# A residual block with tiled fast convolution: where the row transform keeps its scratch, and which adds are done by DMA

## The chip, the cores and the metric

The kernel runs on one core of a Trainium2 chip. A core has five engines that run side by side, each with its own instruction stream: TensorE (matmuls, into PSUM), VectorE (called DVE in the profile), ScalarE (ACT), GpSimd (POOL) and SyncE (SP). SP and POOL issue DMAs; sixteen DMA engines of the core carry them out. The metric is the device time of one execution in microseconds, taken as the median over several runs.

## The reference

The reference is a residual block of a diffusion model: two 3x3 convolutions over 512 channels and a 64x64 image, batch 2, each behind a group normalisation (four groups) and a SiLU. An embedding is added to each channel between the two, and the input at the end.

```python
def conv3(z, w):
    zp = jnp.pad(z, ((0, 0), (0, 0), (1, 1), (1, 1)))
    taps = [jnp.einsum("bchw,oc->bohw", zp[:, :, i:i+H, j:j+W], w[:, :, i, j]) for i in range(3) for j in range(3)]
    ...
h = conv3(_silu(gn(x, g1, be1)), w1)
emb = _silu(t_emb) @ w_emb
h = h + emb.reshape(B, C, 1, 1)
h = conv3(_silu(gn(h, g2, be2)), w2)
return x + h
```

## The kernel before

**The algorithm.** In the vertical direction the convolution is a fast one: four output rows are made from six input rows by six products in place of twelve. So an input tile is first turned, on VectorE and ScalarE, into six *planes* (numbers 0 to 5, 8 rows of 65 elements each, `PL` = 520 elements), each plane is multiplied with its transformed weights on TensorE, and the six products are combined into four output rows. Planes 4 and 5 belong to the *outer rows*: their products are added only to the first and the last of the four output rows. In the horizontal direction some planes have a second fast step, the *nest*: differences of even and odd columns, written to an area of their own (`vnest`).

**Chunks, tiles, units.** The work is cut into eight chunks: layer (2) x image (2) x half of the image (2). A chunk has four input tiles of 128 channels (`ct`) and four units, one for each 128 output channels (`k`). Chunk 0 has no nest (mode N), chunks 1 to 3 have it on planes 0 and 2 (mode 0), chunks 4 to 6 on planes 0 to 3 (mode 1), and chunk 7 on all six. Layer 1's outputs go to a DRAM scratch `h_scr`, layer 2's are added by a DMA from POOL onto `out`, where a DRAM-to-DRAM DMA from SP has put the residual before (the `pre` copies).

**Production.** `prod(c, ct)` (L1163) makes the planes of tile `ct` of chunk `c`, while TensorE works on chunk `c-1`: `load_a` (one of two buffers `AB`), `silu` (ScalarE), then `rows_a` (L624) and `rows_b` (L638). These keep intermediate rows in a scratch `w` of 33 to 34 rows, and write planes 0 to 3 to `X0` or `X1` or to the tile's own area, from where the nest is made. `early` picks one of two orders of the same adds. In the late order planes 4 and 5 first hold a part, and a last add over both planes (1040 elements, the *plane sum*) completes them; where `vacc` is set, that add is an accumulating DMA from POOL inside SBUF. It reads `w`, so `w` can't be written again before it has landed. The scratch is `WB[0]` for all tiles, or one of two (`W2B`) in chunks 5 and 6. The planes and nests of even and odd chunks lie in two areas `VB[0]` and `VB[1]`, `VP` = 4160 elements for each tile; in mode 1 planes 4 and 5 lie elsewhere, in `VX`.

**A unit.** `unit(c, k)` (L823; `unit7` in chunk 7, `last_y` for its last unit) runs the matmuls over the four tiles. ScalarE empties PSUM into `M`, `BT` and the outer-row buffers `OO`; VectorE combines these into the output tile `ys`, one of two. Last come the outer rows: an add of 2 x 520 elements on VectorE (L955), or, where `CFG["oacc"]` of the layer is set, an accumulating DMA from POOL (L953). In layer 1 the tile is then stored, and ScalarE squares and sums it for the next normalisation.

**Order.** Nothing runs in the order of the source. `Plan` collects every operation with a cost, a latency and the ranges that it reads and writes, schedules them (`solve`), and emits them by planned start. So each engine has a fixed order, and an instruction that waits holds up all that is behind it on its engine. A DMA from POOL has a latency of 3.2 us in the plan (L366), beside a time for its size that is reckoned at 150 GB/s when it accumulates.

Of the kernel before, what the change touches and what calls it, by code (L numbers as in the profile page):

```python
# [11 lines left out]
ALU = mybir.AluOpType  # L12
AX = mybir.AxisListType
F32 = mybir.dt.float32
BF16 = mybir.dt.bfloat16
# [162 lines left out]
def _idx(off, dims):  # L178
# [7 lines left out]
RW = 65  # L186
PL = 8 * RW
YF = 4 * PL
AF = 34 * RW
VP = 4160  # L190
KF = 33 * RW
MS = 512
BB, CT, P, NCH, ET = 2, 4, 128, 2, 9
# [6 lines left out]
CFG = {  # L200
    'k0': (D_, D_, D_, D_),
    't0': D_,
    'k': (D_, D_, A_, D_, A_, A_, D_, A_),
    't': (D_, D_, A_, D_, A_, A_, A_, D_),
    's': ((A_, A_, A_), (D_, D_, D_), (D_, A_, A_), (D_, D_, D_), (A_, A_, A_), (A_, A_, D_), (A_, A_, A_), (D_, A_, D_)),
    'oacc': (0, 0),
    'np': 1,
    'pre': 4,
    'wpe': (1, 0, 0, 0),
    'vacc': (1, 0, 0, 1, 0, 1, 1, 1),  # L210
}


# [1 line left out]
def kernel(  # L215
# [14 lines left out]
    o = 0  # L230
    UREG, UM = [], 10304
# [3 lines left out]
    VB = [o, o + 16640 + 2240 + 14928]  # L235
    WB = [o + 16640 + 63]
    Z = o + 16640 + 2240
# [7 lines left out]
    TB = o  # L245
# [7 lines left out]
    X0 = Z + 6912  # L253
    BT0 = Z + 8992
    SD0 = Z + 10016
    O0 = [Z + 11552, Z + 12592, Z + 13632]
    VX = [Z + 16, Z + 6416]
    X1 = Z + 4320
    BT1 = Z + 12880
    W2B = [WB[0], Z + 10721]  # L260
    SD1 = TB

    pool = ctx.enter_context(tc.tile_pool(name="arena", bufs=1))
# [26 lines left out]
    def A(off, dims, dt=None):  # L290
        b = ar[:] if dt is None else ar[:].bitcast(dt)
        n = 1
        for d in dims:
            n *= d[1]
        return R(bass.AP(b.tensor, b.offset + off, [list(b.ap[0])] + [list(d) for d in dims]),
                 ("A", _idx(off, dims)), n)
# [29 lines left out]
    def regs(*rs):  # L326
        return [r.reg if isinstance(r, R) else r for r in rs]

    def tt(out, a, b, op, name=""):
        pl.op("DVE", 0.075 + 0.000521 * out.n, lambda: nc.vector.tensor_tensor(out=out.ap, in0=a.ap, in1=b.ap, op=op),  # L330
              regs(a, b), regs(out), name)
# [23 lines left out]
    def scal(eng, out, a, s, name=""):  # L355
        if eng == "ACT":
            act(out, a, ACT.Copy, scale=s, name=name)
        else:
            ts(out, a, s, name)

    def dma(out, in_, r, w, nbytes, name="", sw=False, acc=False, after=None, lat=None):
        rate = 0.15 if acc else 0.37
        kw = {"accum_op": ALU.add, "max_dma_last_dim": 2080} if acc else {}
        eng = nc.gpsimd if sw else nc.sync
        pl.op("DMA", nbytes / rate * 1e-6 if nbytes > 30000 else 0.1,
              lambda: eng.dma_start(out=out, in_=in_, **kw), regs(*r), regs(*w), name, lat=lat or (3.2 if sw else None), after=after, sw=sw)  # L366

    def memz(eng, out, name="", v=0.0):
        e = getattr(nc, eng)
# [111 lines left out]
    def row_w(w0, w2z, mid, o_um, name):  # L481

        p = A(TB, [[384, 2], [1, 384]])
        if abs(w2z[1] - w2z[0]) < 32768:
            tt(p, A(w0, [[0, 2], [1, 384]], BF16), A(w2z[0], [[w2z[1] - w2z[0], 2], [1, 384]], BF16), ALU.add, name)
        else:
            for i in range(2):
                tt(A(TB + i * 384, [[1, 384]]), A(w0, [[1, 384]], BF16), A(w2z[i], [[1, 384]], BF16), ALU.add, name)
        m = A(mid[0], [[mid[1] - mid[0], 2], [128, 3], [1, 128]], BF16)
        p3 = A(TB, [[384, 2], [128, 3], [1, 128]])  # L490
        tt(A(o_um + 256, [[128, 2], [512, 3], [1, 128]]), p3, m, ALU.add, name)
        tt(A(o_um, [[128, 2], [512, 3], [1, 128]]), p3, m, ALU.subtract, name)
# [13 lines left out]
    def prep_w1(j, ct, eng="ACT"):  # L506
        nm = f"w1_{j}{ct}"
        rb = RAW[rawc[0] % 2]
        rawc[0] += 1
        d = A(rb, [[1, 384]], BF16)  # L510
        dma(d.ap, w1[j][:, 3072 + ct * 384:3072 + (ct + 1) * 384], [], [d], P * 768, nm)
        w0 = UREG[j] + 7168 + ct * 768
        scal(eng, A(rb + 384, [[1, 384]], BF16), d, 2.0, nm)
        scal(eng, A(rb + 768, [[1, 384]], BF16), A(w0 + 384, [[1, 384]], BF16), 4.0, nm)
        row_w(w0, (w0 + 384, rb + 768), (rb, rb + 384), UREG[j] + ct * 1792, nm)

    def nest_w1(j):

# [41 lines left out]
    def mode(c):  # L560
        return "N" if c < CFG["np"] else ("0" if c < 4 else "1")

    acnt = [0]
    acur = {}

    def vplane(c, ct, s):

        v = VB[c % 2] + ct * VP
        if mode(c) == "N":
            return v + s * PL  # L570
        if mode(c) == "0":
            return v + 2048 + {1: 0, 3: 1, 4: 2, 5: 3}[s] * PL
        if c == 7:
            return X1 + s * PL
        return VX[c % 2] + ct * 1088 + (s - 4) * PL

    def vnest(c, ct, kind, s):
        v = VB[c % 2] + ct * VP
        if mode(c) == "0":
            return v + kind * 512 + (s // 2) * 256  # L580
        return v + kind * 1024 + s * 256

    ONEST = [Z + 7440, Z + 10720, None, None]
    LV = VB[0]

    def onest(ct, kind, s):
# [37 lines left out]
    def rows_a(c, ct, w, keng, early):  # L624

        ab = acur[(c, ct)]
        nm = f"row{c}{ct}"
        scal(keng, A(w, [[1, KF]]), A(ab, [[1, KF]]), 4.0, f"k{c}{ct}")
        tt(two(w, 9, 17), two(ab, 1, 26), two(w, 9, 17), SB_, nm)
        s4, s5 = vplane(c, ct, 4), vplane(c, ct, 5)  # L630
        v45 = A(s4, [[s5 - s4, 2], [1, PL]])
        if early:
            tt(two(w, 0, 25), two(w, 0, 25), two(ab, 9, 17), SB_, nm)
            tt(v45, two(w, 0, 25), two(w, 9, 17), AD, nm)
        else:
            tt(v45, two(w, 0, 25), two(ab, 9, 17), SB_, nm)

    def rows_b(c, ct, w, seng, early, vacc=False):  # L638

        ab = acur[(c, ct)]  # L640
        nm = f"rob{c}{ct}"
        s4, s5 = vplane(c, ct, 4), vplane(c, ct, 5)
        rb = 17 if early else 25
        tt(two(w, 0, rb), two(ab, 1, 25), two(ab, 9, 17), SB_, nm)
        t2b = A(w + rb * RW, [[1, PL]])
        scal(seng, t2b, t2b, 2.0, nm)
        Q = two(w, 9, 0)
        SS = two(w, 25, 17) if early else A(s5, [[w + 25 * RW - s5, 2], [1, PL]])
        md = mode(c)
        if md == "N":  # L650
            o = [vplane(c, ct, s) for s in range(4)]
        elif md == "0":
            o = [X0, vplane(c, ct, 1), X0 + PL, vplane(c, ct, 3)]
        else:
            o = [X1 + s * PL for s in range(4)]
        for k, op in ((0, AD), (2, SB_)):
            tt(A(o[k], [[o[k + 1] - o[k], 2], [1, PL]]), Q, SS, op, nm)
        if not early:
            v45 = A(s4, [[s5 - s4, 2], [1, PL]])
            t0 = two(w, 9, 17)  # L660
            if vacc:
                d, t = A(s4, [[1, 2 * PL]]), A(w + 9 * RW, [[1, 2 * PL]])
                dma(d.ap, t.ap, [t, d], [d], P * 4 * PL, f"va{c}{ct}", sw=True, acc=True)
            else:
                tt(v45, v45, t0, AD, nm)
        if md == "N":
            return
        nf = 2 if md == "0" else 4
        xb = X0 if md == "0" else X1
        X = lambda i: A(xb + i, [[RW, 8 * nf], [1, 32]])  # L670
        X2 = lambda i, j: A(xb + i, [[j - i, 2], [RW, 8 * nf], [1, 32]])
        tt(A(vnest(c, ct, 0, 0), [[1, 512 * nf]]), X2(32, 1), X2(33, 0), SB_, nm)
        for kind, op in ((2, SB_), (3, AD)):
            tt(A(vnest(c, ct, kind, 0), [[1, 256 * nf]]), X(33), X(0), op, nm)
        if c == 7:
            if ONEST[ct] is None:
                ONEST[ct] = ab
            xb += 4 * PL
            Y2 = lambda i, j: A(xb + i, [[j - i, 2], [RW, 16], [1, 32]])
            tt(A(onest(ct, 0, 4), [[1, 1024]]), Y2(32, 1), Y2(33, 0), SB_, nm)  # L680
            for kind, op in ((2, SB_), (3, AD)):
                tt(A(onest(ct, kind, 4), [[1, 512]]), A(xb + 33, [[RW, 16], [1, 32]]), A(xb, [[RW, 16], [1, 32]]), op, nm)
# [400 lines left out]
    for i, v in enumerate((-1.0, 2.0, -2.0, 4.0)):  # L1083
# [3 lines left out]
            out=d.ap, in0=ident[:], scalar1=v, scalar2=None, op0=ALU.mult), (), regs(d), "ids")  # L1087
# [42 lines left out]
    def stats1(ct):  # L1130
# [4 lines left out]
        for i in range(4):  # L1135
            pb = VB[0] + (ct * 4 + i) % 3 * VP + 3120
            d = A(pb, [[1, 1040]], BF16)
# [25 lines left out]
    def prod(c, ct):  # L1163
        l = chunks[c][0]
        load_a(c, ct)
        silu(c, ct)
        w = W2B[ct % 2] if 5 <= c < 7 else WB[0]
        rows_a(c, ct, w, CFG["k"][c], False)
        rows_b(c, ct, w, CFG["t"][c], False, CFG["vacc"][c] and (ct < 3 or c < 4))

    memz("gpsimd", A(O0[0] + 32, [[RW, 48], [1, 1]]), "oz")
    opened = []
# [9 lines left out]
    for c in range(8):  # L1182
        l, b, ch = chunks[c]
        for k in range(CT):
# [8 lines left out]
            if c in (1, 2):  # L1193
                for i in range(2):
                    q = (c - 1) * 8 + k * 2 + i
# [99 lines left out]
```

## Time and profile before

| | |
|---|---|
| median of 13 runs | 474.21 us (470.35 to 477.19) |
| the profiled execution | 475.39 us, span of its instructions 473.6 us |
| TensorE clock granted | 0.997 |
| wide adds of 1040 elements on VectorE | 214, mean 696 ns |
| accumulating DMAs inside SBUF, from POOL | 13 of 260 KB, median 4.8 us from issue to landing |
| output DMAs from POOL | 15 of 520 KB, median 5.9 us |
| residual copies from SP | 30 of 260 KB, median 4.9 us |
| DMA queues, share of 16 engines | SP's 48.5%, POOL's 15.1% |

The span runs from the first to the last instruction of the profiled execution; that execution took 1.8 us more than its span. In a row of instructions, the time after the bar is the busy time of the whole group and the mean duration of one of them. Instructions of one engine overlap by some tens of nanoseconds, so a group's busy time is less than count times mean. The brackets of a timeline name the idle time of the engine before the instruction and what ended it.

### The profile page before, as it was taken

To read this page: it belongs to the slowest core of one execution; us is meant where nothing else is said; L and a number is where in the kernel's file an instruction comes from. 1 tells how busy PE (TensorE), PEld (TensorE's weight loads), DVE (VectorE), ACT (ScalarE), POOL (GpSimd) and SP (SyncE) were. 2 spreads that over 40 slices of the span, in tenths; PEclk is the share of its full clock that TensorE was granted. 3 is DMA by queue.
4 is the path that set the end of the run, shared out by engine and by line. 5 is a ranking of instruction groups with operands and counts; after the bars stand their busy time and mean duration, and the time that the engine had idled before them with its cause. 6 is when DMAs were issued, how large, how long until landed. Compare 5 with 4: busy or idle time off the path is not lost. (4 is left out here: it accounts for less than half of the span.)

```text
span 473.6 us, 8317 instructions
## 1 busy us (share of the span) xinstructions
PE 454.1 (96%) x2968; PEld 286.9 (61%) x2968; DVE 438.0 (92%) x843; ACT 372.3 (79%) x588; POOL 45.2 (10%) x77
## 2 busy tenths in 40 slices
PE   6999999999999999999999999999999999989993
PEld 4845554455555555455555577666666666668883
DVE  0599999998999999998999989998999997999997
ACT  5889999389999876699987678859768668666662
POOL 4000000001000000010000000121211111101210
PEclk9999999999999999999999999999999999999998
DMA  8973653265335356674775994996988489435744
GB/s 324 361 262 115 203 163 100 93 222 202 110 113 196 135 144 184 216 252 159 260 269 155 329 297 164 224 266 140 250 191 235 125 206 244 96 104 126 159 79 90
DMA packets 41801, 89.58 MB, mean 189 GB/s; under 512 B 6560, under 2 KB 14624, under 8 KB 41760
## 3 DMA queue, kind: packets, MB, share of 16 engines
q1 hardware_dynamic: 35520, 77.60, 48.5%
q0 software_dynamic: 5952, 11.45, 15.1%
q8 instruction: 23, 0.38, 0.3%
q14 instruction: 18, 0.15, 0.1%
q10 hardware_dynamic: 288, 0.01, 0.0%
HBM read 62.25 MB, written 31.32 MB: 198 GB/s over the span
## 5 line engine op out<-in xcount | busy, mean ns | idle before, releaser
L381 PE MATMUL psum<-ar 128*128 128x256 f16 (+2 forms) x2761 | 435.6, 319 | 6.3 <-ACT ar L353 4.9
L330 DVE TENSOR_TENSOR ar<-ar 128x1040 f16<-128x1040 f16 (+7 forms) x685 | 413.9, 666 | 14.5 <-ACT ar L353 6.8
L381 PEld LDWEIGHTS <-ar 128*128 128x128 f16 (+1 forms) x2797 | 269.6, 98 | 165.8 <-issue 7.3
L353 ACT ACTIVATE ar<-ar 128x384 bf16<-128x384 bf16 (+6 forms) x185 | 159.8, 895 | 51.9 <-DVE ar L330 36.5
L353 ACT ACTIVATE ar<-psum 128x512 f16<-128x512 f32 (+2 forms) x232 | 157.8, 714 | 23.2 <-PE psum L381 10.4
L353 ACT ACTIVATE ar<-ar,fs 128x2112 f16<-128x2112 bf16 (+1 forms) x32 | 68.9, 2155 | 13.6 <-DVE ar L330 6.5
L334 DVE TENSOR_SCALAR ar<-ar 128x512 f16<-128x512 f16 (+2 forms) x73 | 26.3, 381 | 1.6 <-ACT ar L353 1.6
L366 POOL DMA_DIRECT2D out_dram<-ar x15 | 18.5, 1231 | 72.6 <-DVE ar L330 65.6
L381 PE MATMUL psum<-ar,ones_bf 128*128 128x260 bf16 x128 | 19.5, 295 | 4.5 <-DMA ar<-in_x_dram 4.5
L366 POOL DMA_DIRECT2D ar<-ar x13 | 11.9, 912 | 108.7 <-DVE ar L334 50.2
L353 ACT ACTIVATION_READ_ACCUMULATOR ar<-psum 128x1 f32 x100 | 21.7, 217 | 0.0
L381 PEld LDWEIGHTS <-ones_bf 128*128 128x128 bf16 x128 | 13.0, 105 | 10.2 <-issue 3.2
L453 POOL TENSOR_TENSOR fs<-fs 128x1 f32<-128x1 f32 (+1 forms) x7 | 6.5, 923 | 112.9 <-DVE fs L451 112.9
L370 POOL MEMSET ar<- 128x65 f16 (+6 forms) x30 | 5.5, 225 | 121.1 <-PE psum L381 36.7
L1075 DVE SCALAR_TENSOR_TENSOR ar<-psum,ident 128x128 bf16<-128x128 f32 x4 | 1.2, 292 | 9.2 <-PE psum L381 9.2
L353 ACT ACTIVATION_READ_ACCUMULATOR ar<-ar 128x1 f32 x36 | 7.3, 204 | 0.0
L381 PEld LDWEIGHTS psum<-fs,ones_neg 128*128 128x128 f32 x36 | 4.7, 191 | 2.7 <-ACT ar L353 2.4
L381 PE MATMUL psum<-fs,ones_neg 128*128 128x1 f32 (+3 forms) x36 | 4.7, 244 | 1.2 <-ACT ar L353 1.2
L417 ACT ACTIVATE s_sb<-tparm 128x18 bf16<-128x18 bf16 x1 | 0.2, 218 | 3.3 <-DMA tparm<-in_t_emb_dram 3.3
L444 DVE COPY fs<-psum 128x2 f32<-128x2 f32 (+1 forms) x7 | 1.1, 159 | 1.7 <-PE psum L381 1.6
L416 DVE CAST fs<-gparm 128x16 f32<-128x16 bf16 x1 | 0.2, 176 | 2.6 <-DMA gparm<-in_params_dram 2.6
L412 ACT ACT_TABLE_LOAD x1 | 1.3, 1283 | 1.7 <-PEq L1279 1.7
(40 smaller groups left out, 18.8 us busy)
## 6 DMA issues: line engine op xcount, KB each, us to landing
ar<-in_w_dram SPq DMA_DIRECT2D x32, 384.0 KB, 4.9
ar<-in_x_dram SPq DMA_DIRECT2D x16, 552.5 KB, 3.8
h_scr<-ar SPq DMA_DIRECT2D x16, 520.0 KB, 3.0
ar<-h_scr SPq DMA_DIRECT2D x16, 520.0 KB, 4.2
out_dram<-in_x_dram SPq DMA_DIRECT2D x30, 260.0 KB, 4.9
out_dram<-ar POOLq DMA_DIRECT2D x15, 520.0 KB, 5.9
u_scr<-ar SPq DMA_DIRECT2D x16, 384.0 KB, 2.9
ar<-u_scr SPq DMA_DIRECT2D x4, 1536.0 KB, 8.6
```

Source lines behind the costliest of these rows:

```text
L330: pl.op("DVE", 0.075 + 0.000521 * out.n, lambda: nc.vector.tensor_tensor(out=out.ap, in0=a.ap, in1=b.ap, op=op), regs(a, b), regs(out), name)
L334: pl.op("DVE", cost or 0.075 + 0.00026 * out.n, lambda: nc.vector.tensor_scalar(out=out.ap, in0=a.ap, scalar1=s, scalar2=None, op0=ALU.mul ...
L353: lambda: nc.scalar.activation(out=out.ap, in_=a.ap, func=func, scale=sc, **kw), regs(*rr), regs(*ww), name)
L366: lambda: eng.dma_start(out=out, in_=in_, **kw), regs(*r), regs(*w), name, lat=lat or (3.2 if sw else None), after=after, sw=sw)
L370: pl.op("POOL" if eng == "gpsimd" else "DVE", 0.08 + 0.0005 * out.n, lambda: e.memset(out.ap, v), (), regs(out), name)
L381: nc.tensor.matmul(out.ap, lhsT=lhsT.ap, rhs=rhs.ap, start=st, stop=sp, skip_group_check=True)
L412: nc.scalar.activation(out=fs[:, WARM:WARM + 1], in_=fs[:, WARM + 1:WARM + 2], func=ACT.Silu)
L416: nc.vector.tensor_copy(out=fs[:, GB:GB + 4 * CT], in_=gparm[:])
L417: nc.scalar.activation(out=s_sb[:], in_=tparm[:], func=ACT.Silu)
L444: pl.op("DVE", 0.16, lambda: V.tensor_copy(out=F(tot, 2 * n).ap, in_=ps.ap), regs(ps), regs(F(tot, 2 * n)), name, boost=bo)
L453: pl.op("POOL", 0.85 if n == 1 else 1.9, lambda: nc.gpsimd.tensor_tensor(out=F(rs, n).ap, in0=N.ap, in1=F(NEGH, n).ap, op=ALU.pow), regs(N ...
L1075: pl.op("DVE", 0.3, lambda: nc.vector.scalar_tensor_tensor(out=j2.ap, in0=g.ap, scalar=1.0 / HW, in1=ident[:], op0=ALU.mult, op1=ALU.mult, ...
```

## The change

For tiles whose plane sum goes by DMA, the scratch `w` lies in the plane area of the next tile of the same chunk, and the other tiles use the early order, with `w` in the tile's own nest area (mode 1) or in `WB[0]` (mode 0). The last tile has no plane sum by DMA in any chunk. In mode 1 planes 4 and 5 lie right behind the tile's nest (`V1P` = 5184 elements for each tile, areas `VB[0]` and `V1`), and `VX` and `W2B` are gone. In mode 0 planes 0 and 2 also lie in the next tile's area; for the last tile they stay in `X0`, and the pairs of adds are split into single ones. In `prep_w1` a scaled weight is put beside its partner, so that `row_w` needs one add. The settings: outer rows by DMA in both layers; plane sums by DMA in chunks 1 to 6 and not in 7; residual copies tied to a unit 13 back instead of 4; a planned latency of 4.5 us for POOL's DMAs.

```diff
+V1P = 5184
...
-    'oacc': (0, 0),
+    'oacc': (1, 1),
     'np': 1,
-    'pre': 4,
+    'pre': 13,
     'wpe': (1, 0, 0, 0),
-    'vacc': (1, 0, 0, 1, 0, 1, 1, 1),
+    'vacc': (0, 1, 1, 1, 1, 1, 1, 0),
...
-    VX = [Z + 16, Z + 6416]
-    X1 = Z + 4320
-    BT1 = Z + 12880
-    W2B = [WB[0], Z + 10721]
+    V1 = VB[1] + 4 * (VP - V1P)
+    X1 = VB[0] + 4 * V1P
+    BT1 = X1 + 2080
...
-              ... lat=lat or (3.2 if sw else None), after=after, sw=sw)
+              ... lat=lat or (4.5 if sw else None), after=after, sw=sw)
...
-        if abs(w2z[1] - w2z[0]) < 32768:
-            tt(p, A(w0, [[0, 2], [1, 384]], BF16), A(w2z[0], [[w2z[1] - w2z[0], 2], [1, 384]], BF16), ALU.add, name)
-        else:
-            for i in range(2):
-                tt(A(TB + i * 384, [[1, 384]]), A(w0, [[1, 384]], BF16), A(w2z[i], [[1, 384]], BF16), ALU.add, name)
+        tt(p, A(w0, [[0, 2], [1, 384]], BF16), A(w2z[0], [[w2z[1] - w2z[0], 2], [1, 384]], BF16), ALU.add, name)
...
+    def vbase(c, ct):
+        if mode(c) == "1":
+            return (VB[0], V1)[c % 2] + ct * V1P
+        return VB[c % 2] + ct * VP
...
-        if c == 7:
-            return X1 + s * PL
-        return VX[c % 2] + ct * 1088 + (s - 4) * PL
+        return v + 4096 + (s - 4) * PL
...
-            o = [X0, vplane(c, ct, 1), X0 + PL, vplane(c, ct, 3)]
+            xb = X0 if ct == CT - 1 else vbase(c, ct + 1) + 2160
+            o = [xb, vplane(c, ct, 1), xb + PL, vplane(c, ct, 3)]
...
-            tt(A(o[k], [[o[k + 1] - o[k], 2], [1, PL]]), Q, SS, op, nm)
+            if md == "0" and ct == CT - 1:
+                for i, (q, s_) in enumerate(((9, 25), (0, 17))):
+                    tt(A(o[k + i], [[1, PL]]), A(w + q * RW, [[1, PL]]), A(w + s_ * RW, [[1, PL]]), op, nm)
+            else:
+                tt(A(o[k], [[o[k + 1] - o[k], 2], [1, PL]]), Q, SS, op, nm)
...
-        w = W2B[ct % 2] if 5 <= c < 7 else WB[0]
-        rows_a(c, ct, w, CFG["k"][c], False)
-        rows_b(c, ct, w, CFG["t"][c], False, CFG["vacc"][c] and (ct < 3 or c < 4))
+        va = CFG["vacc"][c] and ct < CT - 1
+        w = vbase(c, ct + 1) + 1 if va else (vbase(c, ct) + 1 if mode(c) == "1" else WB[0])
+        rows_a(c, ct, w, CFG["k"][c], not va)
+        rows_b(c, ct, w, CFG["t"][c], not va, va)
```

More of the change, by code (lines that the diff above doesn't have):

```diff
@@ L365, in dma @@
         pl.op("DMA", nbytes / rate * 1e-6 if nbytes > 30000 else 0.1,
-              lambda: eng.dma_start(out=out, in_=in_, **kw), regs(*r), regs(*w), name, lat=lat or (3.2 if sw else None), after=after, sw=sw)
+              lambda: eng.dma_start(out=out, in_=in_, **kw), regs(*r), regs(*w), name, lat=lat or (4.5 if sw else None), after=after, sw=sw)
     def memz(eng, out, name="", v=0.0):
@@ L513, in prep_w1 @@
         scal(eng, A(rb + 384, [[1, 384]], BF16), d, 2.0, nm)
-        scal(eng, A(rb + 768, [[1, 384]], BF16), A(w0 + 384, [[1, 384]], BF16), 4.0, nm)
-        row_w(w0, (w0 + 384, rb + 768), (rb, rb + 384), UREG[j] + ct * 1792, nm)
+        w4 = UREG[j] + ct * 1792
+        scal(eng, A(w4, [[1, 384]], BF16), A(w0 + 384, [[1, 384]], BF16), 4.0, nm)
+        row_w(w0, (w0 + 384, w4), (rb, rb + 384), UREG[j] + ct * 1792, nm)
     def nest_w1(j):
@@ L564 @@
     acur = {}
+    def vbase(c, ct):
+        if mode(c) == "1":
+            return (VB[0], V1)[c % 2] + ct * V1P
+        return VB[c % 2] + ct * VP
     def vplane(c, ct, s):
-        v = VB[c % 2] + ct * VP
+        v = vbase(c, ct)
         if mode(c) == "N":
@@ L572, in vplane @@
             return v + 2048 + {1: 0, 3: 1, 4: 2, 5: 3}[s] * PL
-        if c == 7:
-            return X1 + s * PL
-        return VX[c % 2] + ct * 1088 + (s - 4) * PL
+        return v + 4096 + (s - 4) * PL
     def vnest(c, ct, kind, s):
-        v = VB[c % 2] + ct * VP
+        v = vbase(c, ct)
         if mode(c) == "0":
@@ L581, in vnest @@
         return v + kind * 1024 + s * 256
-    ONEST = [Z + 7440, Z + 10720, None, None]
+    ONEST = [BT1 + 2048, BT1 + 4096, None, None]
     LV = VB[0]
@@ L668, in rows_b @@
         nf = 2 if md == "0" else 4
-        xb = X0 if md == "0" else X1
+        if md == "1":
+            xb = X1
         X = lambda i: A(xb + i, [[RW, 8 * nf], [1, 32]])
@@ L677, in rows_b @@
                 ONEST[ct] = ab
-            xb += 4 * PL
+            xb = vplane(c, ct, 4)
             Y2 = lambda i, j: A(xb + i, [[j - i, 2], [RW, 16], [1, 32]])
```

## The prediction

> **What bounds the kernel now.** I read the page's busy shares first, then the costliest groups, then the same execution cut into stretches, one for each chunk of matrix work, and last the waits and the timeline of the worst stretch.
>
> ```profile
> PE 454.1 (96%) x2968; PEld 286.9 (61%) x2968; DVE 438.0 (92%) x843; ACT 372.3 (79%) x588; POOL 45.2 (10%) x77
> ...
> L330 DVE TENSOR_TENSOR ar<-ar 128x1040 f16<-128x1040 f16 (+7 forms) x685 | 413.9, 666 | 14.5 <-ACT ar L353 6.8
> ```
>
> TensorE is idle for 473.6 - 454.1 = 19.5 us in all: no change to the other engines can give more than that. VectorE is nearly as full. The stretches say where the 19.5 us lie (columns: busy time and count of each engine, granted clock, DMA share, GB/s).
>
> ```profile
> 23.00:97.00 74.00, 72.84 (x395) 35.97 (x394) 73.32 (x159) 65.46 (x133) 1.10 (x2) 1.00 0.49 159
> 97.00:154.00 57.00, 57.00 (x324) 31.59 (x323) 54.51 (x112) 54.67 (x99) 1.40 (x1) 1.00 0.49 167
> 154.00:213.00 59.00, 57.60 (x326) 31.79 (x325) 57.45 (x126) 46.29 (x91) 5.41 (x7) 1.00 0.58 187
> 213.00:270.00 57.00, 57.00 (x323) 31.42 (x321) 54.87 (x96) 50.26 (x85) 1.50 (x9) 1.00 0.71 233
> 270.00:320.00 50.00, 49.30 (x352) 34.24 (x351) 48.22 (x85) 35.73 (x43) 6.96 (x9) 1.00 0.82 239
> 320.00:370.00 50.00, 50.00 (x359) 34.98 (x358) 47.21 (x70) 41.07 (x45) 8.41 (x12) 1.00 0.79 199
> 370.00:423.00 53.00, 49.64 (x352) 34.21 (x351) 48.77 (x75) 35.56 (x41) 8.38 (x11) 1.00 0.70 166
> 423.00:466.00 43.00, 42.10 (x384) 37.42 (x383) 42.64 (x80) 28.27 (x39) 6.02 (x5) 1.00 0.55 110
> 466.00:473.60 7.60, 0.14 (x2) 0.00 (x0) 4.70 (x14) 0.00 (x0) 0.00 (x0) 0.84 0.26 82
> ```
>
> Rows one to eight are chunks 0 to 7. Idle TensorE by row: 1.16, 0, 1.40, 0, 0.70, 0, 3.36, 0.90, then 7.46 after the last matmul; the 4.5 us left lie before the first one. The start waits for loads, and the end is the last tile's output chain on VectorE (5.7 us from the second pair's last add to the last output row) with its store: neither is touched by the change. So what can be won is **7.52 us** in the middle, and nearly half is in chunk 6. What ends those waits is seen there in the timeline:
>
> ```profile
> 391.72 0.57 ACT L353 ACTIVATE ar<-psum 128x512 f16<-128x512 f32 x1
> ...
> 393.78 5.45 PE L381 MATMUL psum<-ar 128*128 128x256 f16 x36 [1.02 <-ACT ar L353]
> ...
> 398.27 1.07 DVE L330 TENSOR_TENSOR ar<-ar 128x1024 f16<-128x1024 f16 x2 [1.51 <-DMA ar<-ar]
> 398.27 1.99 ACT L353 ACTIVATE ar<-ar 128x2145 f16<-128x2145 f16 x1 [2.10 <-DMA ar<-ar]
> ```
>
> TensorE waits for ScalarE to empty a PSUM pair; ScalarE had come late because an instruction ahead of it in its order waited for VectorE. And the last two lines are one accumulating DMA that landed late: VectorE stood 1.51 us for the plane it adds into, ScalarE 2.10 us for the scratch it reads. Over the whole run:
>
> ```profile
> ACT ar L353 <- DMA ar<-ar: 7.4, 4, 2.2
> DVE ar L330 <- DMA ar<-ar: 1.5, 1, 1.5
> ```
>
> **What the change takes off VectorE.** The group of L330 holds 685 adds of 666 ns, 456 us end to end, in 413.9 us of busy time: neighbours overlap, and an add occupies 0.907 of its duration. The 1040-wide form has a mean of 696 ns, so it occupies 0.63 us. With `oacc` on, 28 units (chunks 0 to 6, four each) lose one such add. `vacc` with its bound on `ct` sends 13 tiles to DMA now (4 of chunk 3, 3 each of 5, 6, 7; the page's issues show 13) and 18 afterwards (3 each of chunks 1 to 6): 5 more. The other order of `rows_a`/`rows_b`, taken for tiles that don't use DMA, has six wide adds as the old one had, so it costs nothing. Together 33 x 0.63 = 20.8 us. Against this, three tiles get four 520-wide adds for two wide ones: by the 512-wide row (423 ns) 3 x (4 x 0.384 - 2 x 0.63) = +0.8 us. In weight preparation nine pairs of 384-wide adds (352 ns) become one of 552 ns: 9 x (0.704 - 0.552) x 0.907 = -1.2 us. VectorE: about 21 us less, in a kernel that TensorE bounds, so only where VectorE is late does it count. By stage (a chunk's rows are made during the chunk before): chunk 0 -5.3, chunk 1 -4.1, chunk 2 -1.6 (one add comes back), chunk 3 -4.4, chunks 4 and 5 -2.5 each, chunk 6 -0.6 (four go, three come back for chunk 7), chunk 7 nothing.
>
> **What of it reaches the end.** Chunk 2: VectorE is busy 57.45 of 59 us; relief there and before it is over 5 us, the 1.40 us should mostly go: -1.2. Chunk 4: 48.22 of 50, relief 2.5: -0.6. Chunk 0's 1.16 us lies at its opening, before any outer-row add: 0. Chunk 6 with 7 has 4.26 us and needs a sum of its own: four outer adds -2.5, three plane sums +1.9, the wait for the plane's DMA -1.5 (its cover is now VectorE itself). But the new scratch lies in the plane area that chunk 5 reads till 370 us, where the old one was free at any time: the first tile's first two wide adds, done at 361 us so far, fall into chunk 6: +1.3. Sum -0.8 us of VectorE; also gone are ScalarE's waits for the shared scratch, which stood ahead of evacuations. I take -1.8 for both, between 0 (if the late first tile takes all) and -4.3.
>
> **What it adds.** 33 issues on POOL. The row that is nearest is the same operation, 13 issues at 912 ns: +30 us on an engine busy for 45. Here the Trainium skill speaks against the change: its page "SBUF — State Buffer" (the box on VectorE blocking DMA, in "SBUF: two separate sides", and the figures of the section after it) says that descriptors of POOL-issued DMAs are written through a port that VectorE can lock, and gives 620 ns alone against 3100 ns beside a copy. By that factor 33 issues would be 33 x 0.91 x 5 = 150 us, and the queue would be late everywhere. The trace disagrees for this mix: the 13 lie between 862 and 1087 ns while VectorE is over 90% busy with two-input adds. I take the row.
>
> Landing: from issue, such a DMA took 4.8 us (median on the page; the longest of POOL's was 9.1 us). The page "DMA: Bandwidth & Descriptors", section "Anatomy of one DMA — SWDGE (gpsimd) path", fits 2.0 us plus bytes at 436 GB/s, here 2.6 us. By the rule nobody downstream would wait; by the row the store of the unit (on SP), the square over it (ScalarE, layer 1) and the output DMA (POOL itself) come 4.8 - 0.6 us later than now. What lies behind them: the next loads on SP, the next evacuations on ScalarE, the next plane sums on POOL. The planner now reckons 266 KB / 150 GB/s + 4.5 = 6.3 us, so it puts these behind by more than the median landing, and the output tiles are double buffered over some 24 us. Cost between 0 and the rival below; I take +0.5.
>
> DMA engines: queue 0 moved 11.45 MB in 15.1% of the span's 16 engines, 1.66 us for 266 KB, so 33 add 55 us or 12% to 64%. The earlier residual copies (`pre` 13 instead of 4: nine units sooner on SP) move about 0.13 of a chunk's share from chunks 5 and 6 to 1 and 2. Estimated: chunk 1 0.8, chunk 2 0.8, chunk 3 0.95, chunk 4 0.9, chunk 5 0.8, chunk 6 0.6. Chunk 3 is the tight one; chunks 5 and 6 get no worse.
>
> **Sum.** -1.2 - 0.6 - 1.8 + 0.5 = -3.1 us on the profiled execution's 475.39 us. The median of the runs shown is 474.21, so **471.1 us**, 0.65% less. A difference under 0.5% (2.4 us) can't be told from none here.
>
> **Rivals.** *More of it* (0.15): lateness feeds on itself, and with 21 us of slack all middle idle after chunk 0 goes, 6.4 us: 467.8. For it: every wait there ends with ScalarE behind VectorE. Against: chunk 6, where most of it lies, is hardly relieved.
>
> *Nothing* (0.17): chunks 2 and 4 give 1.8 us, chunk 6 loses as much by the late first tile and three sums back on VectorE: about 474. For it: chunk 1, 3 and 5 have no idle TensorE to win, though they get most of the relief.
>
> *Slower, by sums that land late on in-order engines* (0.23): the place is ScalarE in chunks 0 to 3, whose 16 squares wait for the outer-row DMA. In chunk 6 three gaps of ScalarE of 2.6 to 3.1 us, ended by VectorE, were followed by TensorE gaps of 0.3 to 1.0 us, about a fifth. If DMAs at a share of 0.95 land 3 us after the planned 6.3, 16 x 3 x 0.2 = 9.6 us; less the 3.6 won, 480. It decides from about 1.9 us of overrun on average (6.1 us, 476.7). For it: 9.1 us has been seen, and SP already waits 208 us for VectorE. Against: the square's own place is planned late, and ScalarE is idle for a fifth.
>
> The forecast itself has 0.45. Of it about 0.33 lies beyond -0.5%, with the larger gain and a bit of "nothing" 0.50; slower is the third rival nearly whole and a bit of the second, 0.23; the rest 0.27. The likeliest case alone spans 469 to 473.5; the range over all reaches from 465.5 (all middle idle gone and a low median) to 479 (half of the slower rival).
>
> **What would show it.** VectorE's busy time near 417 us with 33 fewer 1040-wide adds plus 12 of 520; 46 POOL-issued DMAs within the arena at about 0.9 us each; ScalarE's waits for such DMAs in front of the 2145-wide scaling gone; TensorE's idle in chunk 2 under 0.3 us and in chunks 6 and 7 together near 2.5 us; the last 7.5 us as before. Wrong, if ScalarE shows new waits for DMAs before its squares, if the POOL issues lengthen, or if chunk 6 begins with TensorE waiting for planes of its first tile.

## The result and the profile after

| | before | after |
|---|---|---|
| median | 473.69 us (48 runs, 470.35 to 477.75) | 467.72 us (11 runs, 466.23 to 470.33) |
| ratio | 1 | 0.9876, 95% interval 0.9851 to 0.9901 |
| profiled execution / its span | 475.39 / 473.6 us | 467.98 / 466.2 us |

The change makes the kernel 1.24% faster: 5.9 us, about twice the 3.1 us of the forecast. First the busy shares, the group of VectorE's adds, and POOL's accumulating DMAs, from the page of the changed kernel:

```profile
PE 452.2 (97%) x2968; PEld 286.7 (61%) x2968; DVE 418.4 (90%) x807; ACT 373.4 (80%) x588; POOL 84.3 (18%) x110
...
L330 DVE TENSOR_TENSOR ar<-ar 128x1040 f16<-128x1040 f16 (+7 forms) x649 | 393.6, 667 | 27.6 <-ACT ar L353 19.8
...
L366 POOL DMA_DIRECT2D ar<-ar x46 | 50.5, 1115 | 229.3 <-DVE ar L330 110.5
```

VectorE's 19.6 us less (about 21 forecast) and the 46 DMAs are as worked out. Now the stretches, one row for each chunk, then the end (columns as before: busy time and count of PE, PEld, DVE, ACT, POOL, then clock, DMA share, GB/s):

```profile
22.00:96.00 74.00, 72.61 (x396) 35.91 (x396) 71.80 (x153) 68.33 (x138) 7.21 (x7) 1.00 0.62 179
96.00:153.00 57.00, 57.00 (x325) 31.74 (x324) 51.19 (x105) 51.48 (x91) 9.16 (x9) 1.00 0.83 247
153.00:211.00 58.00, 58.00 (x329) 32.05 (x328) 52.33 (x120) 47.24 (x93) 10.62 (x11) 1.00 0.85 243
211.00:267.00 56.00, 56.00 (x319) 31.00 (x318) 48.59 (x85) 47.03 (x82) 8.51 (x15) 1.00 0.85 258
267.00:318.00 51.00, 49.87 (x355) 34.55 (x354) 48.84 (x85) 39.07 (x47) 11.21 (x14) 1.00 0.82 219
318.00:368.00 50.00, 50.00 (x360) 34.97 (x358) 46.84 (x68) 39.66 (x45) 13.36 (x16) 1.00 0.89 204
368.00:417.00 49.00, 49.00 (x352) 34.28 (x351) 47.07 (x74) 37.29 (x42) 10.85 (x14) 1.00 0.68 151
417.00:459.00 42.00, 42.00 (x387) 37.51 (x384) 41.33 (x81) 28.51 (x38) 7.35 (x7) 1.00 0.66 131
459.00:466.20 7.20, 0.17 (x2) 0.00 (x0) 4.28 (x13) 0.00 (x0) 0.00 (x0) 0.78 0.20 74
```

TensorE is idle 1.39 us in chunk 0 and 1.13 us in chunk 4, and not at all in the other six. Chunks 6 and 7 take 49 + 42 us in place of 53 + 43. The middle's idle time went from 7.52 to 2.52 us, and 4.26 of these 5.0 us are of chunks 6 and 7.

What goes on there is seen in ScalarE's scaling of each input tile (2145 elements), the first step of a tile that writes the scratch. Its four instructions for chunk 7 in the timeline, first of the kernel before (the third stands in the prediction):

```profile
359.39 1.99 ACT L353 ACTIVATE ar<-ar 128x2145 f16<-128x2145 f16 x1 [1.22 <-DMA ar<-ar]
...
379.88 3.03 ACT L353 ACTIVATE ar<-ar 128x2145 f16<-128x2145 f16 x3 [2.22 <-DMA ar<-ar]
...
411.08 1.99 ACT L353 ACTIVATE ar<-ar 128x2145 f16<-128x2145 f16 x1 [1.90 <-DMA ar<-ar]
```

and of the changed one:

```profile
367.97 1.98 ACT L353 ACTIVATE ar<-ar 128x2145 f16<-128x2145 f16 x1
...
370.75 1.99 ACT L353 ACTIVATE ar<-ar 128x2145 f16<-128x2145 f16 x1
...
382.98 1.99 ACT L353 ACTIVATE ar<-ar 128x2145 f16<-128x2145 f16 x1
...
391.48 1.99 ACT L353 ACTIVATE ar<-ar 128x2145 f16<-128x2145 f16 x1
```

The first tile does start 9 us later, as forecast, since its scratch lies where chunk 5 still reads. But with one shared scratch in the kernel before the tiles follow at 13 to 20 us, each behind the last use of the scratch by the one before. With a scratch each, two start within 3 us, and the fourth starts 20 us earlier, 26 us before chunk 7 begins instead of 12. My first reading was that the scratch, by letting VectorE work ahead, took the idle time out of chunks 6 and 7. The experiments show that it is not the whole of it.

### The profile page after: what moved, and what is told of

The parts are those of the page before. It is cut to its first block, busy times and chain, and to the rows that moved or that the text cites. A ratio compares the mean times of both kernels' runs of the same rounds, so it can differ in the third digit from the quotient of the medians.

```text
span 466.2 us, 8376 instructions
## 1 busy us (share of the span) xinstructions
PE 452.2 (97%) x2968; PEld 286.7 (61%) x2968; DVE 418.4 (90%) x807; ACT 373.4 (80%) x588; POOL 84.3 (18%) x110
## 4 chain that ended last, share of the span: by engine, by line
PE 77%; DVE 11%; DMA 6%; issue 3%; ACT 3%; DVEq 0%; SPq 0%; ACTq 0%; POOLq 0%
PE psum L381 77%; DVE ar L330 10%; ACT ar L353 3%; DMA ar<-ar 3%; DMA ar<-u_scr 2%; DMA ar<-in_x_dram 1%; DMA ar<-in_w_dram 1%; DVE ar L334 0%; DVEq L1297 0%; SPq L366 0%; DVE fs L444 0%; DVE fs L455 0%; DVE fs L451 0%; DVE fs L446 0%; DVE fs L1026 0%
## 5 line engine op out<-in xcount | busy, mean ns | idle before, releaser
L330 DVE TENSOR_TENSOR ar<-ar 128x1040 f16<-128x1040 f16 (+7 forms) x649 | 393.6, 667 | 27.6 <-ACT ar L353 19.8
L366 POOL DMA_DIRECT2D ar<-ar x46 | 50.5, 1115 | 229.3 <-DVE ar L330 110.5
```

## The experiments

Every kernel was timed in five rounds against the kernel before on the same chip, so the ratios are what is compared between jobs (1% is 4.7 us). Each has its order planned anew, and that matters below. *Idle* is TensorE's idle time between its first and last matmul, in us, read by chunk as above. It comes from one profiled execution of each kernel, and that of a_v7 lay 4.3 us over its median, that of a_nooacc 2.1 us: differences of 1 us in it are not safe.

**One setting at a time.** The theories: (1) VectorE's outer-row adds made chunk 6 late; (2) chunk 7's plane sums by DMA did; (3) the place of the scratch did.

```diff
 b_oacc (from before)
-    'oacc': (0, 0),
+    'oacc': (1, 1),
 b_v7 (from before)
-    'vacc': (1, 0, 0, 1, 0, 1, 1, 1),
+    'vacc': (1, 0, 0, 1, 0, 1, 1, 0),
 a_nooacc (from after)
-    'oacc': (1, 1),
+    'oacc': (0, 0),
 a_v7 (from after)
-    'vacc': (0, 1, 1, 1, 1, 1, 1, 0),
+    'vacc': (0, 1, 1, 1, 1, 1, 1, 1),
```

b_oacc: 

> The kernel before with one setting changed: outer rows of chunks 0 to 6 added by DMA (28 wide adds, 17.7 us, off VectorE); scratch, plane sums and residual copies as before. Theory 1 (the outer-row adds on VectorE made chunk 6 late): most of the 5.9 us gain, 469 to 470.5, and TensorE idle in chunks 6 and 7 falls from 4.3 to under 1.5 us. Theory 2 (chunk 7's plane sums by DMA, with their shared scratch, made chunk 6 late): at most the 1.8 us of chunks 2 and 4, 472 to 473.5, idle in chunks 6 and 7 still over 3 us. Theory 3 (the place of the scratch): as theory 2.

b_v7: 

> The kernel before with one setting changed: chunk 7's three plane sums by DMA become VectorE adds (+1.9 us of VectorE in chunk 6, its wait of 1.5 us for the landing and ScalarE's three waits of about 2 us for the scratch gone). Theory 1: no faster, 473.5 to 476. Theory 2: 3 to 4 us faster, 469.5 to 471, idle in chunks 6 and 7 under 1.5 us. Theory 3: about 473, unless the shared scratch hurts only through chunk 7's DMAs, then as theory 2.

a_nooacc: 

> The changed kernel with the outer rows back on VectorE (28 wide adds, +17.7 us). Theory 1: loses most of the gain, 471 to 474, idle returns in chunks 6 and 7. Theory 2 and 3: keeps the gain of chunk 6, 467.5 to 469.5.

a_v7: 

> The changed kernel with chunk 7's first three plane sums by DMA again, each with its own scratch in the next tile's area. Theory 1: 466.5 to 468.5 (VectorE has 1.9 us less). Theory 2, if it is the landing that hurts: 470 to 471.5, VectorE waits for the accumulating DMA ahead of the nests of planes 4 and 5. Theory 3 (it was the shared scratch, not the landing): 467 to 468.5.

| | median us | ratio (interval) | idle in 6+7 | idle in all chunks | after the last matmul |
|---|---|---|---|---|---|
| before | | 1 | 4.26 | 7.5 | 7.5 |
| after | 467.72 | 0.9876 (0.9851-0.9901) | 0 | 2.5 | 7.0 |
| b_oacc | 482.99 | 1.0207 (1.0163-1.0251) | 2.12 | 12.9 | 7.0 |
| b_v7 | 478.67 | 1.0124 (1.0083-1.0164) | 0.69 | 7.8 | 9.6 |
| a_nooacc | 469.09 | 0.9911 (0.9886-0.9936) | 2.00 | 3.2 | 8.5 |
| a_v7 | 467.18 | 0.9890 (0.9848-0.9932) | 0 | 4.1 | 7.0 |

No theory had this. Taken alone in the old layout, both settings make the kernel *slower*, though each takes idle time out of chunks 6 and 7: it comes back, and more, in chunk 4 (5.9 us in both, 0.7 before), in b_oacc also in chunk 1 (2.9), and in b_v7 also after the last matmul. In the new layout the outer rows are worth 1.7 us by the ratios, whose intervals overlap, and whether chunk 7's sums go by DMA makes no difference to be seen. By the time of the whole kernel, theories 1 and 2 fall as the main cause. For the idle time of chunks 6 and 7 alone theory 2 had it right: it forecast under 1.5 us for b_v7, and 0.69 are left.

What ended those waits says more than their sum. In the kernel before, TensorE's five gaps in chunks 6 and 7 are all ended by ScalarE. ScalarE had itself stood there chiefly for two things: four times for VectorE, 2.6 to 3.1 us each, and 1.9 to 2.2 us for each of three landings, ahead of the scalings. In b_oacc two waits for VectorE of over 0.8 us are left there, 1.9 us at most; the landings cost 5.4, 2.9 and 2.2 us, and 2.12 us of idle remain. In b_v7 the landings are gone, ScalarE still waits for VectorE, and the scalings keep their old pitch (364, 383, 399 and 410 us). Of its ScalarE:

```profile
382.64 1.99 ACT L353 ACTIVATE ar<-ar 128x2145 f16<-128x2145 f16 x1 [0.21 <-DVE ar L330]
...
405.80 0.63 ACT L353 ACTIVATE ar<-ar 128x512 f16<-128x512 f16 x1 [2.54 <-DVE ar L330]
```

and all that is left of TensorE's gaps in the two chunks:

```profile
424.52 7.30 PE L381 MATMUL psum<-ar 128*128 128x256 f16 x64 [0.28 <-DVE ar L330]
...
432.24 7.94 PE L381 MATMUL psum<-ar 128*128 128x256 f16 x71 [0.41 <-DVE ar L330]
```

So the old pitch of the tiles does not by itself make these chunks late; the landings that ScalarE had to wait for at the shared scratch do, as far as one profile of each kernel can show it. VectorE's load is the other half: a_nooacc has its scalings where the changed kernel has them (369, 372, 383 and 394 us), no landing ahead of them, and 2.0 us of idle TensorE that VectorE ends. The longest of these gaps is

```profile
427.59 0.38 PE L381 MATMUL psum<-ar 128*128 128x256 f16 x2 [1.33 <-DVE ar L330]
```

and the chain after its last matmul is 1.5 us longer. In the changed kernel no scaling of chunk 7 waits for a landing, and ScalarE's longest wait for VectorE in the two chunks is 1.6 us; one wait of 3.6 us for an outer row's landing (at 409.6 us) doesn't reach TensorE. And a_v7, with the landings back but a scratch for each tile, has no idle TensorE in these chunks either. How the gain divides between the two can't be told from these runs, since each kernel has its own order.

**The scratch, the DMAs, the planned latency.** Theory 4 is new: the order that comes out of the plan moves the time as much as the change.

```diff
 a_none (from after: every add on VectorE)
-    'oacc': (1, 1), ...  'vacc': (0, 1, 1, 1, 1, 1, 1, 0),
+    'oacc': (0, 0), ...  'vacc': (0, 0, 0, 0, 0, 0, 0, 0),
 a_wb (from after: one shared scratch for tiles whose plane sum goes by DMA)
-        w = vbase(c, ct + 1) + 1 if va else (...)
+        w = (WB[0] if c < 4 else BT1 + 2048) if va else (...)
 b_lat (from before)
-  ... lat=lat or (3.2 if sw else None) ...
+  ... lat=lat or (4.5 if sw else None) ...
 a_lat (from after)
-  ... lat=lat or (4.5 if sw else None) ...
+  ... lat=lat or (3.2 if sw else None) ...
```

a_none: 

> The changed kernel with no add on DMA at all: outer rows and all plane sums on VectorE (46 wide adds back, about +29 us), the new places of scratch and planes kept. If the new placement and its order do it (theory 3), 468 to 471, below the kernel before although VectorE has 8 us more to do than there. If VectorE's load decides (theory 1, and the plane sums count where the outer rows did not), 477 to 485, TensorE idle over 15 us in the middle.

a_wb: 

> The changed kernel with the scratch of all tiles whose plane sum goes by DMA in one place again (shared by the tiles, free to be written early, but each DMA must have landed before the next tile's scaling). Theory 3: loses the gain, 472 to 476, ScalarE or VectorE waits for the accumulating DMAs ahead of the 2145-wide scalings. Theory 1: 467.5 to 469.

b_lat: 

> The kernel before with the planned latency of POOL's DMAs 4.5 us in place of 3.2. Nothing is added or taken away, only the order is planned anew. Theory 4 (the order that comes out of the plan moves the time by as much as the change itself): anything from 469 to 480, off 473.7 by more than 2 us. Theories 1 to 3: 472.5 to 475.

a_lat: 

> The changed kernel with the planned latency back at 3.2 us. Theory 4: off 467.7 by more than 2 us either way. Theory 1 to 3: within 1.5 us of 467.7, or slightly slower if 3.2 us is too short for the 33 more DMAs (ScalarE waits for outer rows before squares), up to 471.

| | median us | ratio (interval) | idle in all chunks |
|---|---|---|---|
| a_none | 474.96 | 1.0000 (0.9978-1.0023) | 5.6 |
| a_wb | 488.59 | 1.0263 (1.0224-1.0302) | 18.4 |
| b_lat | 477.68 | 1.0055 (1.0031-1.0078) | 8.5 |
| a_lat | 475.31 | 0.9994 (0.9968-1.0019) | 8.5 |

a_none lies between its two expectations: the new layout without one DMA add is as fast, within 0.2%, as the kernel before with 13 of them. Against a_nooacc, 18 plane sums by DMA are worth 0.9%, 4.2 us: more than the 28 outer rows, which take more off VectorE. a_wb is the clearest run, and further off than expected: sharing the scratch costs 3.9%, over 18 us. It shares it in chunks 1 to 6 only, where plane sums go by DMA; chunk 7's tiles keep their own, so the run says what 18 such sums need, and nothing of chunk 7's tiles. Chunk 2 in its stretches:

```profile
150.00:154.00 4.00, 3.96 (x18) 1.57 (x16) 2.81 (x6) 4.00 (x9) 1.07 (x1) 1.00 0.81 190
154.00:158.00 4.00, 0.00 (x0) 0.00 (x0) 3.92 (x8) 4.00 (x10) 0.90 (x1) 1.00 0.72 207
158.00:162.00 4.00, 1.46 (x3) 0.42 (x4) 3.90 (x10) 4.00 (x5) 0.00 (x0) 0.57 0.93 249
162.00:166.00 4.00, 0.00 (x0) 0.00 (x0) 3.96 (x11) 2.13 (x4) 1.20 (x1) 0.50 0.95 332
166.00:170.00 4.00, 3.45 (x14) 1.94 (x14) 3.93 (x10) 1.48 (x4) 0.00 (x0) 0.50 1.09 229
```

TensorE has done with chunk 1 at 154 us and stands till 166, but for three matmuls. Its timeline says for what:

```profile
159.76 1.46 PE L381 MATMUL psum<-ar 128*128 128x512 f16 x3 [5.80 <-DMA ar<-ar]
```

The plane sum of the third tile landed at 159.8 us, and the fourth tile could not start before. The scalings of chunk 2's tiles stand at 119.5, 132.9, 149.2 and 160.8 us there, at 120.8, 127.4, 134.0 and 141.0 us in the changed kernel: one turn of the chain scaling, adds, issue, landing, scaling takes 12 to 16 us there, against 7 us with a scratch each, and three turns do not fit between the first scaling and the start of the chunk.

The planned latency: in b_lat and a_lat only the plan's estimate is changed; the instructions are the same in a new order. Back at 3.2 us the changed kernel loses all its gain. ScalarE's waits for accumulating DMAs (us, times, longest), of a_lat, of after, and of a_lat6 (6.0 us, below):

```profile
ACT ar L353 <- DMA ar<-ar: 26.2, 11, 7.1
```
```profile
ACT ar L353 <- DMA ar<-ar: 17.7, 9, 6.2
```
```profile
ACT ar L353 <- DMA ar<-ar: 3.6, 2, 2.3
```

One of them in a_lat, in its timeline about the start of chunk 4:

```profile
269.93 1.20 POOL L366 DMA_DIRECT2D ar<-ar  x1 [14.89 <-issue]
...
273.80 1.94 ACT L353 ACTIVATE ar<-ar 128x2080 fp8e4<-128x2080 f16 x1 [3.15 <-DMA ar<-ar]
...
278.32 2.52 DVE L330 TENSOR_TENSOR ar<-ar 128x1040 f16<-128x1040 f16 x4 [3.41 <-ACT ar L353]
...
282.72 1.58 PE L381 MATMUL psum<-ar 128*128 128x256 f16 x8 [2.77 <-ACT ar L353]
```

POOL issues the outer rows of a unit; the square over that unit (2080 elements) stands 3.15 us for them on ScalarE; evacuations and scalings are queued behind it; VectorE then waits 3.41 us and TensorE 2.77 us. This is the mechanism of the prediction's slower rival, seen in one place; whether it accounts for all of a_lat's loss is not shown. The changed kernel has the wait too, at the same square (the 15th of 16), 2.73 us long:

```profile
265.60 1.99 ACT L353 ACTIVATE ar<-ar 128x2145 f16<-128x2145 f16 x1
...
270.32 1.94 ACT L353 ACTIVATE ar<-ar 128x2080 fp8e4<-128x2080 f16 x1 [2.73 <-DMA ar<-ar]
```

But there one of the two scalings is done ahead of the square (in a_lat both come behind it, at 276.3 and 278.8 us), and TensorE is not idle.

**Own scratch in the old layout, and the rest of the change.**

```diff
 b_w7 (from before)
-        w = W2B[ct % 2] if 5 <= c < 7 else WB[0]
+        w = VB[1] + (ct + 1) * VP + 1 if c == 7 and ct < 3 else (W2B[ct % 2] if 5 <= c < 7 else WB[0])
 a_pre4 (from after)
-    'pre': 13,
+    'pre': 4,
 a_lat6 (from after)
-  ... lat=lat or (4.5 if sw else None) ...
+  ... lat=lat or (6.0 if sw else None) ...
 a_oacc01 (from after)
-    'oacc': (1, 1),
+    'oacc': (0, 1),
```

b_w7: 

> The kernel before with the scratch of chunk 7's first three tiles, whose plane sums go by DMA there, in the next tile's nest area; nothing else is changed, and VectorE's work is the same. If the shared scratch made chunk 6 late: TensorE idle in chunks 6 and 7 (4.3 us before) under 1.5 us, and 470 to 471.5 unless the new plan opens a gap in another chunk. If VectorE's load made it late: 473 to 476, idle in chunks 6 and 7 as before or more, since the first tile can begin only when chunk 5 is done.

a_pre4: 

> The changed kernel with the residual copies tied to a unit 4 back as before instead of 13. If the DMA engines' load in chunks 5 and 6 matters: 469.5 to 472, longer landings there and ScalarE waiting for accumulating DMAs. If the copies were hidden anyway: 467 to 469.

a_lat6: 

> The changed kernel with a planned latency of 6.0 us for POOL's DMAs. If 3.2 us was slow because squares and outputs were planned ahead of the landing: 466.5 to 469, ScalarE's waits for accumulating DMAs below the 17.7 us of the changed kernel. If it was only an unlucky order: anything from 466 to 477 with no relation to those waits.

a_oacc01: 

> The changed kernel with outer rows by DMA in layer 2 only (chunks 4 to 6), on VectorE in layer 1 (16 wide adds back, 10 us, in chunks 0 to 3, where VectorE is 3 to 7 us idle in each). If the 1.4 us that the outer rows are worth come from chunks 6 and 7 alone: 467 to 468.5. If VectorE's relief in layer 1 counts: 469 to 471.

| | median us | ratio (interval) | idle in 6+7 | idle in all chunks |
|---|---|---|---|---|
| b_w7 | 480.66 | 1.0109 (1.0075-1.0142) | 5.36 | 11.0 |
| a_pre4 | 466.43 | 0.9831 (0.9807-0.9854) | 0.14 | 1.5 |
| a_lat6 | 467.58 | 0.9852 (0.9829-0.9875) | 0 | 0.9 |
| a_oacc01 | 467.60 | 0.9854 (0.9827-0.9880) | 0 | 0.8 |

b_w7 is a miss, and it corrects the first reading: an own scratch for chunk 7 is not enough. Its tiles' scalings do come at 374, 376.5, 388 and 402 us, and none of them waits for a landing. But the outer rows are still on VectorE, VectorE itself waits 2.1 us for landings, and chunk 7 begins with 4 us of idle TensorE that VectorE ends:

```profile
427.42 12.77 PE L381 MATMUL psum<-ar 128*128 128x256 f16 x90 [3.98 <-DVE ar L330]
```

In the old layout the own scratch did not help alone; that it needs the fewer adds beside it fits a_nooacc too. a_oacc01: outer rows by DMA in layer 1 make no difference to be seen. a_pre4: the early residual copies don't help, they seem to hurt.

**What was still open.**

```diff
 b_oacc_lat6 (from b_oacc)
-  ... lat=lat or (3.2 if sw else None) ...
+  ... lat=lat or (6.0 if sw else None) ...
 a_wb_lat6 (from a_wb)
-  ... lat=lat or (4.5 if sw else None) ...
+  ... lat=lat or (6.0 if sw else None) ...
 a_pre4_lat6 (from a_lat6), a_pre4_oacc01 (from a_oacc01)
-    'pre': 13,
+    'pre': 4,
```

b_oacc_lat6: 

> The kernel before with outer rows by DMA and a planned latency of 6.0 us. If the short planned latency made outer rows by DMA slow there: 470 to 474, ScalarE's waits for accumulating DMAs from 38.9 us down to under 10. If the shared scratch did it: 478 to 484, waits of ScalarE ahead of 2145-wide scalings remain.

a_wb_lat6: 

> The changed kernel with one shared scratch and a planned latency of 6.0 us. If the place of the scratch is the cause: 482 to 492, chunk 2 again starts late, since its tiles follow each other by scaling, adds, issue and landing. If the plan was: 467 to 474.

a_pre4_lat6: 

> The changed kernel with residual copies 4 units back and a planned latency of 6.0 us: if both take away waits, 465 to 467, idle in the middle under 1.5 us. If the two are only different orders with the same limit, 466 to 468.5.

a_pre4_oacc01: 

> The changed kernel with residual copies 4 units back and outer rows by DMA in layer 2 only: 464.5 to 467 if fewer landings ahead of squares help, idle in the middle about 1 us (chunk 0 alone). TensorE's own time, the start and the last chain leave about 464 as the floor.

a_again (after, unchanged): 

> The changed kernel as it is, beside the next one: 466.5 to 468.5.

a_pre4_again (a_pre4, unchanged): 

> The changed kernel with the residual copies 4 units back, on the same chip. If early copies hurt (they fill the DMA engines in chunks 1 to 4, where outer rows and plane sums must land): 1 to 2 us below the run beside it. If they make no difference: within 0.7 us of it.

| | median us | ratio (interval) | idle in all chunks |
|---|---|---|---|
| b_oacc_lat6 | 480.33 | 1.0111 (1.0066-1.0157) | 10.2 |
| a_wb_lat6 | 484.80 | 1.0216 (1.0170-1.0262) | 15.5 |
| a_pre4_lat6 | 467.03 | 0.9831 (0.9791-0.9872) | 1.4 |
| a_pre4_oacc01 | 465.82 | 0.9818 (0.9770-0.9867) | 1.8 |
| a_again | 468.08 | 0.9870 (0.9838-0.9903) | 2.1 |
| a_pre4_again | 466.26 | 0.9828 (0.9799-0.9857) | 1.4 |

a_wb_lat6 settles that plane sums by DMA need a scratch each: with 6.0 us planned the shared one still costs 3.7% against a_lat6, 12.9 us of idle in chunk 2 alone. b_oacc_lat6 has the time of its second expectation and nearly the waits of its first: ScalarE's waits for these DMAs fall from 38.9 to 10.2 us (5.3 of them still ahead of 2145-wide scalings), and chunk 4's idle is gone, but VectorE now waits 8.1 us for them, chunks 0, 1 and 7 are late, and the kernel is still 1.1% slower than before. So half of b_oacc's loss went with the planned latency, and the rest stays with the old layout. Residual copies 4 units back were faster in all four pairs of kernels, by 0.2 to 0.45%; the intervals overlap in each, so it is likely and not certain that this part of the change costs time. a_pre4, a_pre4_lat6 and a_pre4_oacc01 can't be told apart; each beats the kernel before by 1.7 to 1.8%.

How far is a single difference to be trusted? b_lat changes nothing but an estimate inside the plan and moves the time by 0.55%. Differences of this size between two of these kernels, that of the outer rows (0.35%) among them, may be of the order and not of the edit. In the changed kernel the estimate alone moves it by 1.2%, as much as the whole gain, so the plane sums' 0.9% may be of the order too. Only those of the scratch (3.9 and 3.7%) are well above this.

## Why the prediction was off by half

- *TensorE bounds, 7.52 us can be won in the middle*: right. 5.0 of them were.
- *VectorE: about 21 us less*: right, 19.6 us.
- *Chunk 2, "the 1.40 us should mostly go: -1.2"*: all of it went, -1.40. *Chunk 4, -0.6*: 0.70 became 1.13 in the profile above. In a_again, a second profile of the same kernel, it is 0 and chunk 2 has 0.67 instead: gaps of about 1 us move from run to run, and only their sum (2.5 and 2.1 us with chunk 0's) says something. *Chunk 0: 0*: +0.23. The new stalls, taken at +0.5, can't be told from these gaps.
- *Chunks 6 and 7, "I take -1.8 for both, between 0 (if the late first tile takes all) and -4.3"*: **this is the step that failed**: -4.26, the far end. With -0.8 us for VectorE's work, about -1.0 was left for ScalarE's waits at the shared scratch, and that was too little. b_v7 takes those waits away (with VectorE's one of 1.5 us) and the idle time of the two chunks falls by 3.57 us, where the prediction's terms (+1.9 - 1.5 - 1.0) would give 0.6; part of that may be its own order, in which idle time came up elsewhere. The charge of +1.3 for a late first tile did not show in the changed kernel, whose chunks 6 and 7 have no idle time. In b_w7, with the outer rows on VectorE, TensorE does wait for VectorE as chunk 7 begins; whether the late tile or VectorE's other work is behind that is open. b_w7 and a_none show the other half: own scratch in chunk 7 with the outer rows on VectorE, or in chunks 4 to 7 with all adds there, makes the kernel no faster than before.
- *"neither is touched by the change", of the start and the end*: not quite for the end. The chain after the last matmul took 7.46 us before, 7.02 after. It was 8.5 in a_nooacc and 9.6 in b_v7, where VectorE has more to do, but also 8.0 in a_lat6, which has the changed kernel's instructions, so the order moves it as well.
- *33 issues at the row's 0.91 us, not at five times that*: the row was the better guide. 18 plane sums took 0.95 us each, 28 outer rows, which are two pieces in a row, 1.22 us; POOL is busy 39 us more instead of 30.
- *Landing 4.8 us*: the median is 4.8 us after too. *DMA shares 0.8, 0.8, 0.95, 0.9, 0.8, 0.6 in chunks 1 to 6*: 0.83, 0.85, 0.85, 0.82, 0.89, 0.68.
- *The slower rival*: its mechanism exists and a_lat shows it. The sign named for it came true in the changed kernel as well: four squares wait for their DMA, 0.85 to 6.21 us and 11.7 us together, where none did before. TensorE was not idle for them. With 3.2 us planned in place of 4.5, which I had taken for a detail of the slower case, the whole gain is gone. *"More of it"*, 467.8 us, had the right time, but put it down to VectorE's slack alone, which in the old layout (b_oacc, b_oacc_lat6) made the kernel slower.

The profiled executions differ by 7.4 us, more than the medians: that of before lay 1.7 us over its median. 5.4 us of it is idle TensorE (7.52 to 2.52 in the middle, 7.46 to 7.02 after it), and the rest is busy time of the same 2968 matmuls (454.1 and 452.2 us), whose cause is open. Against the forecast's -3.1 us, chunks 6 and 7 gave 2.5 more, and 0.2 came from chunk 2, 0.5 from the new stalls, 0.4 from the end and 1.9 from the busy time; chunks 4 and 0 took back 1.3.

## What to carry to other kernels

A scratch that is shared by successive tiles and last read by a DMA can cost more than the waits that a profile shows at it, since what stands behind them in order is late too, and it can limit how far production runs ahead (a_wb). Look at what ended the waits of the first instruction that writes it, and at the pitch of its starts, tile after tile; the pitch alone proves nothing (b_v7). When adds move to DMA, look at what is ordered behind the instructions that wait for the landing. In this kernel the planner's estimate of the landing was worth as much (1.2%) as the adds themselves.

## What the runs showed of the hardware

TensorE's clock can fall by half for about 3.4 us after gaps that are not long. In a_v7 it stood 1.51 us at 304 us (columns as above, the clock is the third last):

```profile
304.00:306.00 2.00, 0.49 (x5) 0.42 (x5) 2.00 (x4) 1.41 (x3) 0.12 (x1) 1.00 1.14 183
306.00:308.00 2.00, 2.00 (x13) 1.44 (x13) 1.36 (x2) 2.00 (x4) 0.00 (x0) 0.57 1.05 185
308.00:310.00 2.00, 2.00 (x11) 1.34 (x10) 1.85 (x7) 2.00 (x2) 1.33 (x2) 0.58 0.25 46
```

From 306.3 to 309.7 us the granted clock is 0.5 (1.00 in the stretches of 2 us before and behind): 1.7 us more on top of the gap, in a TensorE that looks busy. The records show the same 3.4 us after gaps of 2.2 us (b_lat) and 2.5 us (a_none), and 13.7 us in a_wb. The kernel before had a gap of 1.98 us at 421 us and b_oacc_lat6 one of 2.35 us at 96 us, and both kept their clock, so the length of one gap alone doesn't decide. The Trainium skill ("TensorE: Matmul & The Clock Gate", Part 1) tells of windows of 3.4 us, which agrees with the duration; it warns of idle gaps over some 3.4 us, and here 1.5 us was enough once. In a_v7 the stall thus cost about twice its length, 1.51 + 1.7 us, and the idle time of the profile doesn't show the second part.
